# Last batch's ff stage: six of eight pairs of ff tiles by seven half-size products

## The chip, the core and the metric

The kernel runs on one core of one Trainium2 chip. The engines are PE (TensorE, with PEld for its weight loads), DVE (VectorE), ACT (ScalarE), POOL (GpSimd) and SP (SyncE, which here only issues DMAs). The metric is the device time in microseconds; lower is better. Three runs of the kernel before gave 210.69, 211.95 and 211.96 us, a median of 211.95.

## What is computed

Four batches of sparse attention (8 heads, 768 positions, head size 64), and on its output `x` (3072 x 512) an ff layer with a quick gelu:

```python
def _moe_ref(x, w_in, w_out):
    h = x @ w_in                               # 512 -> 2048
    g = h * (1.0 / (1.0 + np.exp(-1.702 * h)))
    return (g @ w_out).astype(np.float32)      # 2048 -> 512
```

Attention for each position: the keys within 15 positions, and the maximum of each block of 32 keys, against the values and the mean of each block of values.

## The kernel before, in words

The whole program is one list of words, `ORDER` (lines 35 to 110). A loop (lines 931 to 933) splits each word at its dots and calls the step of that name. Every engine is wrapped (`_Ordered`, line 18), so that each instruction is tied behind the one issued before it on its engine; line 28 is the helper's line and stands for nearly all instructions in the profile. The order on each engine's queue is thus meant to be the order of the words.

The stages of the four batches overlap: while PE computes the output products of batch b, the attention of batch b+1 is woven between them, and then the ff stage of batch b+1 follows. The words that matter here:

- `lk.b.h` (line 190): POOL issues the load of one head of keys. `lq` and `lv` do so for queries and values.
- `xk.s.g.e` (line 649): SP issues a DMA transpose of half of a group of four heads of keys into `kx`; it needs the four loads of that group. `xq` does so for queries.
- `v.b.half.p` (line 674): attention values of two heads. `nn.half.g` (line 697) normalizes four heads on DVE into `x2`, and `d.half.g` (line 715) has SP transpose them by DMA into `xTT[half][g]`, the ff input of positions `half` and model columns `g` (256 each). Each half has 384 positions.
- `f.half.nt.k...` (line 721): ff matmuls of tile nt (128 of 2048 ff columns), one for each `ko` named (`k0123`); ko 0 and 1 read `xTT[half][0]`, 2 and 3 `xTT[half][1]`. All are 128x128 by 128x384. `g.half.nt` (line 737) is the gelu on ACT into `gTb`.
- `gs.j.n.what` (line 740): sums and differences of gelu outputs, on DVE, or on POOL with `.g`.
- `p.t.what` (line 829): the output layer by seven half-size products, each 8 matmuls of 256 columns, with tiles named poA, poB and poC. `x.t.what` (line 852) takes a product out of PSUM, on ACT (`.a`) or DVE (`.d`; additions always on DVE). `o.t.half...` (line 869) has SP store a finished row block. `osb` has three buffers.
- `gate.2` (line 909): POOL copies one column of `xTT[1][1]`, so that loads behind it on POOL's queue wait for that transpose.
- `U`, `W`, `P`, `S`, `H`, `P7` (lines 751 to 814): an ff stage by seven products. In the kernel before only `P7.0` is in the list, which closes the pool `even` (attention buffers of even batches, line 425 onward) at the very end; the others are defined and not used.

The ff stage of each batch, the last too, is 16 tiles x 2 halves x 4 ko = 128 matmuls. PSUM has four single banks (0 to 3) and two double ones (`40`/`41`, `50`/`51`; `42` and `52` mean both halves).

Of the kernel before, what the change touches and what calls it, by code (L numbers as in the profile page):

```python
# [82 lines left out]
f.0.0.k23 lk.3.6 g.0.1 g.0.9 g.0.8 f.1.1.k0123.0 f.1.8.k0123.1 g.0.0 f.1.9.k0123.3 g.1.1 g.1.9 g.1.8 f.1.0.k0123.2
f.0.10.k0123.0 g.0.10 gate.2 g.1.0 gs.0.2.2 xk.1.1.0 f.1.2.k0123.1 gs.0.2.0.d gs.0.2.1 xk.1.0.1 f.1.10.k0123.3 g.1.2
o.1.1.1.0.2 g.1.10 lq.3.6 f.0.2.k0123.2 gs.0.2.3 lv.3.5.1 f.1.3.k0123.1 vm.3.52 g.1.3 xk.1.1.1 g.0.2 xk.1.0.0
o.1.2.1.0.2 f.0.13.k0123.0 f.0.3.k0123.2 f.1.11.k0123.3 f.0.12.k0123.1 g.0.3 g.0.13 g.1.11 xa.0.1 f.0.4.k0123.2 xq.1.1
f.1.12.k0123.3 lq.3.1 f.0.11.k0123.0 g.0.4 gs.2.2.2.g g.0.12 f.1.5.k0123.1 g.0.11 lq.3.2 vb xa.1.1 xq.1.0 f.0.5.k0123.2
g.1.5 g.1.12 ha.3.3.0 f.1.4.k0123.0 kR.1.d g.1.4 f.1.14.k0123.3 g.0.5 f.1.6.k0123.1 g.1.14 gs.2.2.0 ha.3.1.0
f.0.14.k0123.0 gs.2.2.1.g f.0.6.k0123.2 g.1.6 f.1.13.k0123.3 g.0.14 f.1.7.k0123.1 f.0.15.k0123.0 g.1.13 g.0.6 ka.1.d
f.1.15.k0123.3 f.0.7.k0123.2 s.3.0.1.42 gs.2.2.3 g.1.7 gs.6.1.0 gs.6.1.1 g.1.15 gs.4.2.0 g.0.15 gs.6.1.3 s.3.0.0.52  # L90
sd.3.1.0 g.0.7 gs.6.1.2 p.0.2.3 gs.7.1.0 p.0.1.2 X ha.3.0.0 e.0.1 p.1.2.0 e.0.0 x.0.1.d m.0.1 gs.7.1.1.g p.0.5.1
s.3.0.2.52 e.0.2 gs.4.2.1 x.0.5.d s.3.0.3.42 e.0.3 p.0.6 x.0.2.a gs.4.2.2 p.1.1.3 x.0.6.d s.3.1.1.42 gs.7.1.2 gs.7.1.3
s.3.1.0.52 gs.4.2.3 e.1.0 p.0.7 x.1.1.d p.0.3 ha.3.2.0 e.1.1 m.0.2 s.3.1.3.42 e.1.3 s.3.1.2.52 p.1.6 x.1.2.a x.0.3.a
m.0.0 x.0.7.a m.1.3 m.0.3 sd.3.0.0 p.1.5.1 v.3.0.2.40 e.1.2 v.3.0.0.50 v.3.0.3.41 v.3.0.1.51 o.2.0.0.0.2 G x.1.6.a m.1.2
p.0.4 p.1.7 m.1.0 x.0.4.a nn.0.0 x.1.5.d m.1.1 x.1.7.a p.2.1.2 p.1.3 nn.0.1 o.2.0.1.0.2 x.2.1.d p.1.4 d.0.0 v.3.1.2.40
v.3.1.3.41 x.1.3.a v.3.1.0.50 v.3.1.1.51 x.1.4.d d.0.1 p.2.5.1 p.2.6 nn.1.0 nn.1.1 x.2.6.a o.2.1.0.0.2 x.2.5.d p.2.2.3
x.2.2.a p.2.7 x.2.7.a p.2.3 p.2.4 f.0.1.k01.0 x.2.4.a f.0.1.k23 f.0.9.k01.3 f.0.0.k01.2 x.2.3.a f.0.9.k23 f.0.8.k01.1
f.0.0.k23 f.0.8.k23 o.2.1.1.0.2 g.0.9 g.0.0 g.0.8 d.1.0 d.1.1 f.1.9.k0123.3 f.1.0.k0123.2 g.0.1 f.1.8.k0123.1
f.1.1.k0123.0 g.1.9 g.1.0 f.0.2.k0123.2 f.1.11.k0123.3 g.1.8 g.0.2 f.1.2.k0123.1 g.1.1 f.0.10.k0123.0 g.1.11
f.1.13.k0123.3 g.1.2 f.1.3.k0123.1 g.0.10 f.0.3.k0123.2 g.1.13 f.1.10.k0123.3 g.0.3 f.0.11.k0123.0 f.0.4.k0123.2 g.1.3  # L100
g.1.10 f.1.12.k0123.3 o.2.2.0.0.2 gs.2.2.0.d g.0.4 g.0.11 f.1.4.k0123.1 gs.2.2.1.g g.1.12 f.0.12.k0123.0 f.1.14.k0123.3
o.2.2.1.0.2 g.0.12 gs.0.2.0.d f.0.5.k0123.2 g.1.4 f.1.5.k0123.1 f.0.13.k0123.0 g.0.5 f.0.6.k0123.2 gs.2.2.2.g g.1.5
g.0.13 g.1.14 f.1.6.k0123.1 f.0.14.k0123.0 g.0.6 g.1.6 gs.6.1.0.d f.0.7.k0123.2 g.0.7 gs.0.2.2.g gs.4.2.0.g
f.1.7.k0123.1 g.0.14 f.1.15.k0123.3 g.1.7 gs.0.2.1.g f.0.15.k0123.0 gs.4.2.1 g.0.15 gs.6.1.1 gs.6.1.2.d gs.2.2.3 p.0.1.2
g.1.15 gs.7.1.0 gs.7.1.1.g p.0.5.1 x.0.1.d p.0.2.0 p.0.6 x.0.6.a x.0.2.a gs.6.1.3 gs.4.2.2.d x.0.5.d gs.7.1.2 p.1.1.3
p.0.7 p.2.2.0 x.0.7.a x.1.1.a gs.0.2.3.d gs.7.1.3.g gs.4.2.3 p.0.4 x.0.4.a p.0.3 x.0.3.a p.1.2.2 x.1.2.a p.1.6
o.3.0.0.0.2 x.1.6.a p.1.5.1 x.1.5.d o.3.0.1.0.2 p.2.1.2 x.2.1.d p.1.3 x.2.2.a p.1.7 x.1.3.a p.2.6 x.2.6.d x.1.7.a
# [6 lines left out]
def kernel(  # L114
# [633 lines left out]

    seven = {}

    def seven_pool(n):
# [4 lines left out]
        seven["pool"] = p7
        seven["w"] = p7.tile([128, 4, 2, n * 128], F16, name="ws7", tag="ws7", bufs=1)
        seven["x"] = p7.tile([128, 4, 2, HALF], F16, name="xs7", tag="xs7", bufs=1)

    def w_sum7(what, j0, n, eng):  # L760
        c = slice(j0 * 128, (j0 + n) * 128)
        d = slice(d_ff // 2 + j0 * 128, d_ff // 2 + (j0 + n) * 128)
# [12 lines left out]
    def product7(j, what, where=None):  # L775
        c = slice(j * 128, j * 128 + 128)
        d = slice(d_ff // 2 + j * 128, d_ff // 2 + j * 128 + 128)
        w, x = seven["w"], seven["x"]
        lhs, rhs, name = {
            1: (w_in_sb[:, 0:2, c], xTT[0][0], "A"),  # L780
            2: (w_in_sb[:, 2:4, c], xTT[0][1], "C"),
            6: (w[:, 1, :, c], x[:, 1], "A"),
            5: (w[:, 0, :, c], x[:, 0], "B"),
            7: (w[:, 2, :, c], x[:, 2], "A"),
            3: (w[:, 3, :, c], xTT[1][1], "B"),
            4: (w_in_sb[:, 2:4, d], x[:, 3], "A")}[what]
# [8 lines left out]
    def taken7(j, what, eng):  # L795

        ph = seven[j, "at", what]
        if what in (1, 6, 5):
            if what == 1:
                seven[j, "h"] = seven["pool"].tile([128, 2, HALF], F32, name="h7", tag="h7")  # L800
            if what == 5:
                seven[j, "r"] = seven["pool"].tile([128, HALF], F32, name="r7", tag="r7")
            copy(eng, {1: lambda: seven[j, "h"][:, 0], 6: lambda: seven[j, "h"][:, 1],
                       5: lambda: seven[j, "r"]}[what](), ph)
# [159 lines left out]
```

## Time and profile before

| | |
|---|---|
| median of 3 runs | 211.95 us (210.69 to 211.96) |
| the profiled execution's own time | 211.7 us |
| its span | 210.0 us |
| PE busy | 200.4 us, 95% |
| DVE, ACT, POOL busy | 130.8, 114.3, 109.1 us |
| ff stage of batch 2 (PE) | from 123.10 us |
| ff stage of batch 3, the last (PE) | 167.26 to 188.06 us |
| output products of the last batch (PE) | 188.06 to 206.42 us |

The page of a profile gives busy time for each engine, the chain of work that ended last, and groups of instructions with their count, busy time, mean duration and the idle time before them with what ended it. A name such as `ph<-xT,w_in_sb` is output from inputs. In a timeline a row holds the start, the length and the number of like instructions; `SPq` and `POOLq` rows are the issuing of DMAs. Consecutive matmuls overlap, so their pace is read from the length of a run of them, not from the mean of one. The chain's rows are start, length, engine and tile.

### The profile page before, as it was taken

To read this page: it belongs to the slowest core of one execution; us is meant where nothing else is said; L and a number is where in the kernel's file an instruction comes from. 1 tells how busy PE (TensorE), PEld (TensorE's weight loads), DVE (VectorE), ACT (ScalarE), POOL (GpSimd) and SP (SyncE) were. 2 spreads that over 40 slices of the span, in tenths; PEclk is the share of its full clock that TensorE was granted. 3 is DMA by queue.
4 is the path that set the end of the run, shared out by engine and by line. 5 is a ranking of instruction groups with operands and counts; after the bars stand their busy time and mean duration, and the time that the engine had idled before them with its cause. 6 is when DMAs were issued, how large, how long until landed. Compare 5 with 4: busy or idle time off the path is not lost.

```text
span 210.0 us, 5880 instructions
## 1 busy us (share of the span) xinstructions
PE 200.4 (95%) x2440; PEld 145.8 (69%) x2440; DVE 130.8 (62%) x311; ACT 114.3 (54%) x227; POOL 109.1 (52%) x157
## 2 busy tenths in 40 slices
PE   7998798999999999999999999999999999999993
PEld 5656554667887886556788865657888865668882
DVE  5577873798997871168997822694888500166342
ACT  2473885659666736676764336567670157671100
POOL 7999972399982998448949422431000000863000
PEclk9999999999999999999999999999999999999998
DMA  4999999999999999999999999939215920000214
GB/s 67 162 166 189 209 213 221 182 144 122 99 134 199 156 177 183 130 126 141 148 166 204 142 227 180 187 29 169 50 53 139 160 105 0 0 3 0 100 53 150
DMA packets 96458, 27.74 MB, mean 132 GB/s; under 512 B 85024, under 2 KB 93488, under 8 KB 96432
## 3 DMA queue, kind: packets, MB, share of 16 engines
q0 software_dynamic: 70800, 13.64, 82.7%
q1 hardware_dynamic: 25632, 13.74, 33.2%
...
q14 instruction: 7, 0.06, 0.1%
...
## 4 chain that ended last, share of the span: by engine, by line
PE 79%; POOL 12%; DMA 5%; issue 1%; DVE 1%; SPq 0%; POOLq 0%; DVEq 0%
PE ph L28 36%; PE poA L28 19%; PE poB L28 10%; PE poC L28 5%; PE ps_s L28 3%; PE ps_av L28 3%; DMA vw<-vw 2%; POOL mk L28 2%; DMA out_dram<-osb 2%; POOL v0n L28 2%; POOL w_in_sb L28 2%; POOL kb L28 2%; POOL kx L28 2%; POOL qb L28 1%; PE ps_t L28 1%
## 5 line engine op out<-in xcount | busy, mean ns | idle before, releaser
L28 PE MATMUL ph<-xT,w_in_sb 128*128 128x384 f16 x512 | 86.1, 326 | 0.4 <-DVE osb L28 0.4
L28 ACT ACTIVATE gT<-ph 128x384 f16<-128x384 f32 x128 | 56.1, 495 | 30.6 <-PE ph L28 29.9
L28 PEld LDWEIGHTS <-w_in_sb 128*128 128x128 f16 x512 | 49.2, 98 | 32.4 <-issue 0.9
L28 PEld LDWEIGHTS <-gs 128*128 128x128 f16 x384 | 36.5, 98 | 4.6
L28 DVE TENSOR_TENSOR gs<-gT 128x768 f16<-128x768 f16 (+1 forms) x36 | 17.5, 498 | 29.1 <-ACT gT L28 29.0
L28 POOL TENSOR_TENSOR gs<-gs,gT 128x768 f16<-128x768 f16 (+1 forms) x6 | 8.8, 1461 | 41.8 <-PE ph L28 32.7
...
L28 ACT ACTIVATE a_sb<-ps_s 128x768 bf16<-128x768 f32 x32 | 24.8, 808 | 9.5 <-PE ps_s L28 9.3
L28 PEld LDWEIGHTS <-gT 128*128 128x128 f16 x288 | 27.3, 98 | 3.6
...
L28 PE MATMUL poA<-ws,gs 128*128 128x256 f16 x192 | 24.8, 273 | 0.0
...
L28 DVE TENSOR_TENSOR a_sb<-a_sb,mk 128x768 bf16<-128x768 bf16 x28 | 14.7, 550 | 3.0 <-ACT a_sb L28 2.2
L28 DVE TENSOR_TENSOR x<-ps_av,rc 128x768 f16<-128x768 f32 (+1 forms) x18 | 15.6, 869 | 0.6
L28 ACT ACTIVATE s<-poA 128x256 f32<-128x256 f32 x14 | 5.4, 382 | 19.3 <-PE poA L28 18.6
L28 PE MATMUL poB<-ws,gs 128*128 128x256 f16 x96 | 12.5, 273 | 0.0
L28 PE MATMUL poC<-w_out_sb,gT 128*128 128x256 f16 x96 | 12.5, 273 | 0.0
L28 PE MATMUL poA<-w_out_sb,gT 128*128 128x256 f16 x96 | 12.4, 273 | 0.0
L28 PE MATMUL poB<-w_out_sb,gs 128*128 128x256 f16 x96 | 12.4, 273 | 0.0
L28 PE MATMUL poA<-ws,gT 128*128 128x256 f16 x96 | 12.3, 273 | 0.0
L28 DVE TENSOR_REDUCE ka<-kx 128x48 bf16<-128x1536 bf16 x4 | 7.0, 1750 | 7.4 <-DMA kx<-kb 7.4
...
## 6 DMA issues: line engine op xcount, KB each, us to landing
...
kb<-in_k_dram POOLq DMA_DIRECT2D x24, 96.0 KB, 6.0
qb<-in_q_dram POOLq DMA_DIRECT2D x24, 96.0 KB, 5.0
...
```

What stands on the lines that cost most here:

```text
L28: r = f(*a, **kw)
```

## The change

In the last batch's ff stage the tiles 2 to 7 are paired with 10 to 15. With `w_in` and the input each cut in four quarters, the four quarter blocks of a pair's output (two tiles, two halves) come from seven products of half the depth (two ko) instead of eight. Each product is two matmuls of 128x384, so a pair takes 14 matmuls instead of 16. Tiles 0, 1, 8 and 9 stay as they were.

- `P7.6.2` closes `even` and opens the pool `seven` (weights sums `ws7`, input differences `xs7`, three `r7` buffers of 384 f32). It stands in batch 2's ff stage now, and the `P7.0` at the end is gone.
- `W.0` to `W.3`: the sums of quarters of `w_in` for the six pairs, 128 x 1536 f16, on DVE; three in batch 2's ff stage and one in batch 3's attention.
- `U.0` to `U.3`: differences of the inputs, 128 x 768 f16, on DVE, at the start of the last ff stage.
- For each pair j: `P.j.1` opens the left part of a double bank X, `P.j.5` its right part. `S.j.1` copies the left part from PSUM into another PSUM bank A (DVE); `P.j.2` is then added onto the left part by PE, `P.j.6` onto A. `S.j.5` (ACT) copies the right part to SBUF (h). `S.j.6` (DVE) writes A + h onto the right part in PSUM, and `P.j.3` is added onto that; `P.j.7` is added onto A, `S.j.7` (DVE) adds A to h, and `P.j.4` is added onto A. The gelus: `H.j.0` over both parts of X (768), `H.j.1` over A, `H.j.2` over h (384 each).
- The eight `gs` sums of the last batch that were on POOL are on DVE.
- The list of words from the end of batch 1's output products on is in another order, also for batch 2's ff stage and batch 3's attention, though with the same steps.

```diff
-    def seven_pool(n):
+    def seven_pool(n, j0):
         even.close()
         if not n:
             return
-        p7 = ctx.enter_context(tc.tile_pool(name="seven", bufs=2, side="right", reuse_waits="tile"))
+        p7 = ctx.enter_context(tc.tile_pool(name="seven", bufs=1, side="right", reuse_waits="tile"))
...
-        opens = where is not None
-        if opens:
-            seven[j, name] = bank(where, F32, "ph" + name)[:, 0:HALF]
-        seven[j, "at", what] = ph = seven[j, name]
+        if where is not None:
+            X = seven[j, "X"] = bank(where, F32, "phX")
+            seven[j, "l"], seven[j, "r"] = X[:, 0:HALF], X[:, 512:512 + HALF]
         for i in range(2):
-            pe.matmul(out=ph, lhsT=lhs[:, i], rhs=rhs[:, i], start=(opens and i == 0), stop=(i == 1),
-                      skip_group_check=True)
+            pe.matmul(out=seven[j, name], lhsT=lhs[:, i], rhs=rhs[:, i], start=(what in (1, 5) and i == 0),
+                      stop=(i == 1), skip_group_check=True)
...
+    def taken7(j, what, eng, where=None):
+        if what == 1:
+            seven[j, "A"] = bank(where, F32, "phA")[:, 0:HALF]
+            copy(eng, seven[j, "A"], seven[j, "l"])
+        elif what == 5:
+            seven[j, "h"] = seven["pool"].tile([128, HALF], F32, name="r7", tag="r7", bufs=3)
+            copy(eng, seven[j, "h"], seven[j, "r"])
         else:
-            t_ = {2: lambda: seven[j, "h"][:, 0], 3: lambda: seven[j, "h"][:, 1], 7: lambda: seven[j, "r"]}[what]()
-            dve.tensor_tensor(out=t_, in0=ph, in1=t_, op=ALU.add)
+            to = seven[j, "r"] if what == 6 else seven[j, "h"]
+            eng.tensor_tensor(out=to, in0=seven[j, "A"], in1=seven[j, "h"], op=ALU.add)
```

The words at the start of batch 2's ff stage, after the change (the last values of batch 2 are `v.2.1.3`):

```
... v.2.1.3.51 d.0.0 o.1.1.0.0.2 p.2.6 d.0.1 p.2.2.3 ... p.2.7 nn.1.0 f.0.1.k01.0 f.0.1.k23 nn.1.1 ... d.1.0
... f.0.9.k01.3 f.0.9.k23 p.2.4 d.1.1 o.1.2.0.0.2 ... f.0.8.k01.1 f.0.8.k23 lk.3.6 g.0.9 g.0.1 P7.6.2
xk.1.1.0 x.2.4.a f.1.9.k0123.3 f.0.0.k01.2 gate.2 xk.1.0.1 f.1.1.k0123.0 ...
```

and at the start of the last one (the last values of batch 3 are `v.3.1.3`):

```
... v.3.1.3.41 p.1.4 p.2.5.1 f.0.1.k01.0 nn.1.0 x.1.4.d x.2.6.a nn.1.1 f.0.1.k23 p.2.2.3 x.2.5.d o.2.1.0.0.2 o.2.1.1.0.2
d.1.0 p.2.3 p.2.7 g.0.1 x.2.2.a x.2.3.a U.0.d x.2.7.a P.2.1.42 f.0.8.k01.1 d.1.1 f.0.8.k23 P.2.5 P.3.1.52 P.3.5 g.0.8
U.2.d f.1.1.k0123.0 S.2.5.a U.1.d f.1.8.k0123.1 g.1.1 p.2.4 g.1.8 o.2.2.0.0.2 S.2.1.d.0 S.3.5.a U.3.d P.2.2 P.2.6
S.3.1.d.1 P.3.6 P.3.2 S.2.6.d P.2.3 S.3.6.d P.2.7 S.2.7.d f.0.9.k01.3 P.3.3 P.3.7 S.3.7.d x.2.4.a P.2.4 H.2.0 ...
```

On PE, DVE, ACT and POOL the built program follows the list. On SP it does not at one place, in batch 2: the instructions of SP's queue stand there in this order, before and after the change (`kx` in the group of heads 4 to 7 is `xk.1.1.0`, in heads 0 to 3 `xk.1.0.1`):

```
before: d.0.0  o.1.1.0  d.0.1  d.1.0     d.1.1  o.1.2.0   xk.1.1.0  xk.1.0.1  o.1.1.1  xk.1.1.1  xk.1.0.0  o.1.2.1  xq  xq
after:  d.0.0  o.1.1.0  d.0.1  xk.1.1.0  d.1.0  xk.1.0.1  d.1.1     o.1.1.1   o.1.2.0  xk.1.1.1  xk.1.0.0  o.1.2.1  xq  xq
```

In both programs `xk.1.1.0` waits for the semaphore that `lk.3.6` raises when it has landed, and `lk.3.6` stands at the same place of POOL's queue. PE's queue has 24 instructions fewer: 12 matmuls and 12 weight loads.

More of the change, by code (lines that the diff above doesn't have):

```diff
@@ L83 @@
[L83 to L107, printed above, removed]
@@ new lines @@
+xk.1.1.0 x.2.4.a f.1.9.k0123.3 f.0.0.k01.2 gate.2 xk.1.0.1 f.1.1.k0123.0 g.0.8 W.0.2.6.d g.1.1 f.1.8.k0123.1 lq.3.6
+g.1.9 W.2.2.6.d f.0.0.k23 f.0.10.k0123.0 f.1.10.k0123.3 g.1.8 lv.3.5.1 o.1.1.1.0.2 lq.3.1 g.0.0 f.1.2.k0123.1 xk.1.1.1
+f.1.0.k0123.2 g.1.10 g.0.10 g.1.2 xk.1.0.0 o.1.2.1.0.2 f.1.11.k0123.3 f.0.11.k0123.0 lq.3.2 g.1.0 g.1.11 g.0.11
+f.0.4.k0123.2 xq.1.1 xa.0.1 f.0.12.k0123.1 g.0.4 f.1.12.k0123.3 g.0.12 g.1.12 f.0.3.k0123.2 g.0.3 f.1.3.k0123.1 xq.1.0
+f.1.4.k0123.0 f.0.2.k0123.2 g.1.3 g.1.4 g.0.2 f.1.5.k0123.1 f.0.13.k0123.0 xa.1.1 vm.3.52 g.1.5 g.0.13 f.0.5.k0123.2
@@ new lines @@
+f.1.13.k0123.3 ka.1.d ha.3.3.0 f.0.15.k0123.0 g.0.5 gs.2.2.0 W.1.2.6.d gs.2.2.2.g f.0.6.k0123.2 kR.1.d g.0.15 g.1.13
+f.1.6.k0123.1 gs.0.2.2 f.1.14.k0123.3 ha.3.1.0 g.0.6 g.1.6 vb g.1.14 gs.6.1.2 f.0.7.k0123.2 gs.4.2.0 gs.6.1.0
+f.1.7.k0123.1 gs.2.2.1.g g.1.7 gs.4.2.1 gs.2.2.3 f.1.15.k0123.3 f.0.14.k0123.0 sd.3.1.0 gs.0.2.0.d s.3.0.0.52 g.1.15
+gs.6.1.1 s.3.0.1.42 g.0.7 p.0.1.2 g.0.14 ha.3.0.0 gs.7.1.0 x.0.1.d p.0.5.1 X e.0.0 gs.7.1.1.g p.0.2.3 e.0.1 gs.0.2.1
+p.0.6 gs.7.1.2 gs.6.1.3 s.3.1.0.52 ha.3.2.0 gs.4.2.2 e.1.0 x.0.2.a x.0.5.d s.3.0.3.42 p.1.2.0 gs.4.2.3 p.1.1.3
@@ new lines @@
+s.3.0.2.52 W.3.2.6.d e.0.3 gs.0.2.3 m.0.0 x.0.6.d sd.3.0.0 e.0.2 s.3.1.1.42 gs.7.1.3 x.1.1.d m.0.3 p.0.3 x.0.3.a e.1.1
+p.0.7 m.1.0 s.3.1.3.42 s.3.1.2.52 e.1.2 x.0.7.a p.1.5.1 o.2.0.0.0.2 e.1.3 p.1.6 p.0.4 m.0.1 m.0.2 m.1.1 v.3.0.2.40
+v.3.0.3.41 m.1.3 x.0.4.a x.1.5.d v.3.0.0.50 x.1.2.a v.3.0.1.51 o.2.0.1.0.2 x.1.6.a nn.0.0 p.2.1.2 p.1.7 G x.2.1.d nn.0.1
+m.1.2 x.1.7.a p.1.3 p.2.6 x.1.3.a v.3.1.2.40 v.3.1.0.50 d.0.0 v.3.1.1.51 d.0.1 v.3.1.3.41 p.1.4 p.2.5.1 f.0.1.k01.0
+nn.1.0 x.1.4.d x.2.6.a nn.1.1 f.0.1.k23 p.2.2.3 x.2.5.d o.2.1.0.0.2 o.2.1.1.0.2 d.1.0 p.2.3 p.2.7 g.0.1 x.2.2.a x.2.3.a
@@ new lines @@
+U.0.d x.2.7.a P.2.1.42 f.0.8.k01.1 d.1.1 f.0.8.k23 P.2.5 P.3.1.52 P.3.5 g.0.8 U.2.d f.1.1.k0123.0 S.2.5.a U.1.d
+f.1.8.k0123.1 g.1.1 p.2.4 g.1.8 o.2.2.0.0.2 S.2.1.d.0 S.3.5.a U.3.d P.2.2 P.2.6 S.3.1.d.1 P.3.6 P.3.2 S.2.6.d P.2.3
+S.3.6.d P.2.7 S.2.7.d f.0.9.k01.3 P.3.3 P.3.7 S.3.7.d x.2.4.a P.2.4 H.2.0 P.4.1.42 P.4.5 H.3.0 H.2.1 S.4.5.a P.3.4
+S.4.1.d.0 H.3.1 P.5.1.52 P.5.5 P.4.2 H.2.2 P.4.6 S.5.5.a f.0.9.k23 S.5.1.d.1 P.5.6 S.4.6.d g.0.9 H.3.2 P.5.2 P.4.3 P.4.7
+S.5.6.d f.0.0.k01.2 S.4.7.d P.5.3 H.4.0 P.5.7 P.4.4 P.6.1.42 gs.2.2.0 H.5.0 S.5.7.d P.6.5 H.4.1 P.7.1.52 S.6.5.a P.5.4
@@ new lines @@
+H.5.1 S.6.1.d.0 f.0.0.k23 P.7.5 g.0.0 gs.2.2.2 S.7.1.d.1 P.6.6 H.4.2 P.6.2 f.1.0.k0123.2 S.7.5.a gs.2.2.1 H.5.2 S.6.6.d
+g.1.0 P.7.6 P.7.2 S.7.6.d P.6.7 P.6.3 f.1.9.k0123.3 P.7.3 gs.4.2.0 H.6.0 S.6.7.d P.7.7 P.6.4 gs.0.2.2 g.1.9 S.7.7.d
+gs.4.2.1 gs.0.2.0 H.7.0 H.7.2 gs.6.1.2 H.6.1 H.6.2 p.0.1.2 x.0.1.d P.7.4 H.7.1 p.1.1.3 gs.6.1.0 gs.4.2.3 gs.7.1.0
+p.0.2.0 x.0.2.a p.0.5.1 gs.7.1.1 gs.0.2.1 gs.6.1.1 gs.0.2.3 gs.4.2.2 gs.7.1.3 p.2.2.0 gs.2.2.3 x.1.1.a gs.7.1.2 p.0.6
+x.0.5.d o.2.2.1.0.2 gs.6.1.3 x.0.6.a p.1.6 p.0.7 p.0.3 x.0.7.a p.0.4 x.0.3.a x.0.4.a p.1.5.1 p.1.2.2 x.1.2.a x.1.6.a
@@ L110 @@
+x.1.5.d o.3.0.0.0.2 o.3.0.1.0.2 p.1.7 x.1.7.a p.2.1.2 p.1.3 x.2.1.d p.2.6 x.1.3.a o.3.1.0.0.2 p.2.5.1 x.2.6.d x.2.5.a
+p.2.7 p.2.3 x.2.2.a p.1.4 x.2.7.a o.3.2.1.1.2 p.2.4 x.2.3.a x.1.4.d o.3.2.0.0.2 o.3.1.1.0.2 x.2.4.d o.3.2.1.0.1
 """
@@ L754, in seven_pool, with w_sum7 @@
             return
-        p7 = ctx.enter_context(tc.tile_pool(name="seven", bufs=2, side="right", reuse_waits="tile"))
[L756 to L762, printed above, removed]
+        p7 = ctx.enter_context(tc.tile_pool(name="seven", bufs=1, side="right", reuse_waits="tile"))
+        seven["pool"], seven["j0"] = p7, j0
+        seven["w"] = p7.tile([128, 4, 2, n * 128], F16, name="ws7", tag="ws7")
+        seven["x"] = p7.tile([128, 4, 2, HALF], F16, name="xs7", tag="xs7")
+    def w_sum7(what, j, n, eng):
+        c = slice(j * 128, (j + n) * 128)
+        d = slice(d_ff // 2 + j * 128, d_ff // 2 + (j + n) * 128)
         a11, a12, a21, a22 = (w_in_sb[:, 0:2, c], w_in_sb[:, 2:4, c], w_in_sb[:, 0:2, d], w_in_sb[:, 2:4, d])
-        w = seven["w"][:, :, :, c]
+        w = seven["w"][:, :, :, (j - seven["j0"]) * 128:(j + n - seven["j0"]) * 128]
         a, b, op = ((a21, a22, ALU.add), (w[:, 0], a11, ALU.subtract), (a11, a21, ALU.subtract),
@@ L777, in product7 @@
         d = slice(d_ff // 2 + j * 128, d_ff // 2 + j * 128 + 128)
-        w, x = seven["w"], seven["x"]
+        o = slice((j - seven["j0"]) * 128, (j - seven["j0"]) * 128 + 128)
+        w, x = seven["w"][:, :, :, o], seven["x"]
         lhs, rhs, name = {
[L780 to L785, printed above, removed]
+            1: (w_in_sb[:, 0:2, c], xTT[0][0], "l"),
+            2: (w_in_sb[:, 2:4, c], xTT[0][1], "l"),
+            6: (w[:, 1], x[:, 1], "A"),
+            5: (w[:, 0], x[:, 0], "r"),
+            7: (w[:, 2], x[:, 2], "A"),
+            3: (w[:, 3], xTT[1][1], "r"),
@@ L795, in taken7 @@
[L795 to L804, printed above, removed]
-        else:
-            t_ = {2: lambda: seven[j, "h"][:, 0], 3: lambda: seven[j, "h"][:, 1], 7: lambda: seven[j, "r"]}[what]()
-            dve.tensor_tensor(out=t_, in0=ph, in1=t_, op=ALU.add)
+            pe.matmul(out=seven[j, name], lhsT=lhs[:, i], rhs=rhs[:, i], start=(what in (1, 5) and i == 0),
+                      stop=(i == 1), skip_group_check=True)
@@ L809, in gelu7 @@
     def gelu7(j, which):
         k2 = j + NT // 2
-        o, i = ((gTb[:, j], lambda: seven[j, "h"].rearrange("p a c -> p (a c)")),
-                (gTb[:, j, 0:HALF], lambda: seven[j, "h"][:, 0]), (gTb[:, j, HALF:S], lambda: seven[j, "h"][:, 1]),
-                (gTb[:, k2, 0:HALF], lambda: seven[j, "A"]), (gTb[:, k2, HALF:S], lambda: seven[j, "r"]))[which]
+        o, i = ((gTb[:, j].rearrange("p (h c) -> p h c", h=2),
+                 lambda: seven[j, "X"].rearrange("p (h c) -> p h c", h=2)[:, :, 0:HALF]),
+                (gTb[:, k2, 0:HALF], lambda: seven[j, "A"]), (gTb[:, k2, HALF:S], lambda: seven[j, "h"]))[which]
@@ L856, in taken @@
             name = {1: "s1", 6: "s2", 5: "s5"}[what]
-            p_ = seven.get("pool", snap) if what == 1 else snap
-            t_ = now[t, name] = p_.tile([128, N1], F32, name=name, tag=name)
+            t_ = now[t, name] = snap.tile([128, N1], F32, name=name, tag=name)
             copy(eng, t_, po)
```

10 lines of the change are left out of this document (4 added, 6 removed).

## Prediction, on record before the change was run

> **What bounds the kernel now.** I read the page first (busy shares, chain), then the chain of waits by time, then busy time by window, and last the timelines of SP, POOL and PE around the edges of the ff stages.
>
> ```profile
> span 210.0 us, 5880 instructions
> PE 200.4 (95%) x2440; PEld 145.8 (69%) x2440; DVE 130.8 (62%) x311; ACT 114.3 (54%) x227; POOL 109.1 (52%) x157
> PE 79%; POOL 12%; DMA 5%; issue 1%; DVE 1%; SPq 0%; POOLq 0%; DVEq 0%
> ```
>
> ```profile
> 161.04 0.88 PE ps_av L28 x48
> ...
> 166.39 0.87 PE poA L28 x8
> 167.26 20.80 PE ph L28 x128
> 188.06 0.87 PE poA L28 x8
> ...
> 204.66 1.76 PE poA L28 x16
> 206.42 0.02 issue
> 206.44 0.42 DVE osb L28
> ```
>
> TensorE is the bound, and in the last batch it is the bound without a break. The chain's pieces join end to end: the last attention values end at 161.92 (call it V), six half-size output products follow, the 128 ff matmuls take 20.80 us (0.1625 us each), and output products at 0.87 us per eight run to 206.42. A matmul removed there shortens the run by its 0.1625 us, if nothing makes PE wait.
>
> ```profile
> 145.00:165.00 20.00, 20.00 (x329) 17.09 (x322) 15.72 (x36) 10.29 (x16) 0.91 (x1) 1.00 0.43 108
> 167.30:188.10 20.80, 20.80 (x130) 12.58 (x129) 3.75 (x6) 13.56 (x31) 8.32 (x5) 1.00 0.09 30
> ```
>
> Columns are the window, its length, then busy time of PE, weight loads, DVE, ACT and POOL. In the last ff stage DVE is idle for 17 of 20.8 us, ACT for 7.
>
> **The change, part by part.** *Matmuls.* A pair of ff tiles takes 16 matmuls of 384 columns (two tiles, two halves, four ko), and by seven products 14. Six pairs save 12: 12 x 0.1625 = 1.95 us. All are on the path.
>
> *Work added beside them.* DVE gets a copy and two additions of 384 f32 for each pair, four differences of the inputs (U, 768 f16), four of w_in (W, 1536 f16), and the eight gelu sums that POOL did. ACT's four gelus per pair become one of 768, two of 384 and a copy of 384.
>
> ```profile
> L28 ACT ACTIVATE gT<-ph 128x384 f16<-128x384 f32 x32 | 14.0, 491 | 7.2 <-PE ph L28 7.2
> L28 DVE TENSOR_TENSOR gs<-gT 128x768 f16<-128x768 f16 x3 | 1.6, 552 | 11.4 <-ACT gT L28 11.4
> L28 DVE TENSOR_TENSOR gs<-gT 128x384 f16<-128x384 f16 x4 | 1.5, 384 | 6.2 <-ACT gT L28 6.2
> L28 DVE TENSOR_TENSOR osb<-poC,s 128x256 f32<-128x256 f32 x3 | 1.3, 425 | 1.5 <-PE poC L28 1.5
> ```
>
> ```profile
> L28 DVE TENSOR_TENSOR x<-ps_av,rc 128x768 f16<-128x768 f32 x4 | 3.8, 958 | 0.1
> ```
>
> ```profile
> L28 ACT ACTIVATE a_sb<-ps_s 128x768 bf16<-128x768 f32 x32 | 24.8, 808 | 9.5 <-PE ps_s L28 9.3
> ```
>
> A 384-column f32 operation out of PSUM lies between 0.425 (256) and 0.958 us (768), by a straight line 0.56. A PSUM target is in no row; I price it as an SBUF one. DVE: 18 x 0.56 + 4 x 0.55 = 12.3 us, plus 6 x 0.55 + 2 x 0.38 = 4.1 of sums: beside the 3.75 it has, about 20 us, spread over the 18.85 us stage and the product stage behind it. ACT: 6 x (0.81 + 3 x 0.49) + 8 x 0.49 = 17.6 us. Both fit, because two pairs run interleaved: while pair 3 copies, pair 2 multiplies. What is not covered is the start. PE reaches the product that needs U.0 after five output products and ten ff matmuls, V + 5 x 0.87 + 10 x 0.1625 = V + 6.0.
>
> ```profile
> 163.22 2.55 SPq L28 DMA_TRANSPOSE xT<-x  x2
> ```
>
> ```profile
> xT<-x SPq DMA_TRANSPOSE x1, 2.8
> ```
>
> ```profile
> xT<-x SPq DMA_TRANSPOSE x2, 3.6
> ```
>
> Input d.1.0 was issued at V + 1.3 and landed 2.8 us later, d.1.1 at V + 2.6 and 4.4 (the median of the two is 3.6). Now d.1.0 stands behind a store that needs x.1.4, itself behind nn.1.0: V + 2.1. It lands at V + 4.9 to 5.7, U.0 takes 0.55, and PE waits 0 to 0.35. D.1.1 follows at V + 3.3 and lands at V + 6.1 to 7.7; then DVE's U.2, U.1, S.2.1, U.3 and S.3.1 (0.55 each) end at V + 8.9 to 10.5, and P.3.6, which needs the last, stands 18 ff matmuls and one output product behind U.0's product, at V + 9.8: 0 to 0.7. Together, since the second wait shrinks by the first, 0 to 0.9; I take 0.35. W.0 and W.2 (0.93 us each, on the line through 0.38 and 0.55) fall into a DVE gap of 6.7 us (row below); W.1 and W.3 lie where DVE has a fifth of its time free, 0. If that cover were gone, W.3 would cost its 0.93.
>
> *The SP queue, which the diff does not show.* In the built program the d.1.0 and d.1.1 transposes of batch 2 no longer stand ahead of the key transposes of batch 3: the order is d.0.1, xk.1.1.0, d.1.0, xk.1.0.1, d.1.1. And xk.1.1.0 waits for the last key load, lk.3.6. This is a new wait, and behind it in SP's queue stand both ff inputs of batch 2, two output stores and the other key transposes; POOL's gate.2, with three loads behind it, waits for d.1.1.
>
> ```profile
> 116.74 0.89 POOL L28 DMA_DIRECT2D kb<-in_k_dram  x1
> ...
> 118.58 3.91 SPq L28 DMA_TRANSPOSE xT<-x  x3
> ...
> 123.10 8.61 PE L28 MATMUL ph<-xT,w_in_sb 128*128 128x384 f16 x52 [0.41 <-DVE osb L28]
> ...
> 123.41 0.34 SPq L28 DMA_DIRECT2D out_dram<-osb  x1
> ...
> 124.36 3.33 SPq L28 DMA_TRANSPOSE kx<-kb  x2
> 124.58 0.19 POOL L28 CAST gate<-xT 128x1 bf16<-128x1 f16 x1 [6.95 <-DMA xT<-x]
> ...
> 130.05 1.03 DVE L28 TENSOR_TENSOR gs<-gT 128x768 f16<-128x768 f16 x2 [6.67 <-ACT gT L28]
> ```
>
> ```profile
> kb<-in_k_dram POOLq DMA_DIRECT2D x1, 96.0 KB, 5.1
> ```
>
> ```profile
> xT<-x SPq DMA_TRANSPOSE x1, 4.6
> ```
>
> ```profile
> L28 SPq DMA_TRANSPOSE xT<-x x4: 1211/1244/1257, 114.0 to 121.3; - x4
> ...
> DMA to landing us min/median/max: 3.2/4.3/5.7
> ```
>
> ```profile
> L28 SPq DMA_TRANSPOSE kx<-kb x4: 1217/1438/1939, 124.4 to 130.0; - x4
> ```
>
> The durations min/median/max are in ns. The first of the three transposes from 118.58 landed 4.6 us after its issue, the last 3.2. Before: d.1.1 was issued at 121.25 and landed 3.2 us later, 124.45 (the gate opened at 124.58), ahead of its first use at 123.10 + 16 x 0.1625 = 125.70. So it was hidden by 1.2 us. After: lk.3.6 keeps its place on POOL, was issued at 116.74 and lands 5.1 later, 121.84. Then xk.1.1.0, d.1.0, xk.1.0.1 hold SP for 1.44 + 1.24 + 1.44 us (medians) and three small steps of 0.05: d.1.1 is issued at 126.15 and lands at 129.35, by its own 3.2. PE now has only 12 ff matmuls ahead of the tile that needs it, and that tile's two first ko use d.1.0. The same amount of work was done before at 125.70 - 4 x 0.1625 + 2 x 0.1625 = 125.38. PE stands until 129.4: 4.0 us later, the former 0.41 wait included. Nothing gives it back, since PE is the bound from there to the end. Low end: 1.22, 1.21, 1.22 on SP and a landing of 2.8 (last batch): 128.5, 3.1 us. The key transposes come earlier for no gain, since PE sets when the next scores run. High end: SP was free at 123.75 before its first key transpose and began it at 124.36, so 0.6 more, then 1.94, 1.26, 1.94 and 4.6: 132.4, 7.0 us. I take 4.0, by the median rows.
>
> *The end* (206.42 to the profiled execution's 211.7 us) keeps its order: 0.
>
> **Sum:** 211.7 - 1.95 + 0.35 + 4.0 = 214.1. The profiled execution is 0.25 us below the median of 211.95, so against that median 214.35; I forecast **214.3 us**, 1.1% slower.
>
> **Rivals.** *The transposes stay hidden* (other side). Lk.3.6 lands so early that SP does not stand: the place is xk.1.1.0 on SP, the price of the wait 0, and the 0.41 goes too: 211.95 - 1.95 + 0.35 - 0.41 = 209.95. The point from which it decides: the sum turns at a shift of 1.6 us, d.1.1 landed by 127.0, lk.3.6 by 119.4. Against it: issued at 116.74, it would have to land within 2.7 us, and the quickest key load took 3.7.
>
> ```profile
> DMA to landing us min/median/max: 3.7/6.0/9.1
> ```
>
> *The clock falls in the hole.* PE would stand from about 124.5 until d.1.0 lands (issued at 123.4, 126.6), run two matmuls, and stand 2.5 us more.
>
> ```profile
> 1.30 4.45 PE L28 MATMUL ps_h<-warm 128*128 128x256 bf16 x20 [1.30 <-DVE warm L28]
> ...
> 34.69 0.73 PE L28 MATMUL ps_av<-vw,a_sb 128*64 128x65 bf16 x35 [0.77 <-DMA vw<-vw]
> ```
>
> At the start 256-column matmuls took 4.45 / 20 = 0.22 us where eight take 0.87 later, 0.109 each: twice as long for 4.45 us, a loss of 2.27. Later the longest single wait shown is 0.77 and leaves the rate alone. If the hole brings the slow rate back for as long, 214.3 + 2.3 = 216.6. [...]
>
> *The pairs are not covered.* A slow PSUM-to-PSUM copy, or ACT late with a gelu that frees a bank, costs each of six pairs 0.35 us (0.56 against 0.33 of matmuls beside it, and a hand-over): 214.3 + 2.1 = 216.4. For it: ACT at 17.6 of 18.85 us. Against: DVE has three steps per pair against 2.3 us of matmuls.
>
> *The change does not do what it says:* the built program has 12 matmuls and 12 weight loads fewer, so no.
>
> **How the numbers follow.** Main case 0.70 (by the bounds 211.95 - 1.95 + 0 + 3.1 = 213.1 to 211.95 - 1.95 + 0.9 + 7.0 = 217.9); hidden 0.10; clock 0.12; pairs 0.08. About 1% is what a measurement of this kernel can tell from no change: 209.83 and 214.07. Of the main case 0.42 lies above 214.07 and 0.28 within; clock and pairs lie above; of the hidden case 0.06 is within and 0.04 below. Faster 0.04, same 0.34, slower 0.62. The range, 211.5 to 217.5, takes in a shift half hidden, and leaves out the hidden case and the uppermost tenth.
>
> **What would show it.** Right: in the profile after, SP's timeline has a kx transpose between the second and third xT, waiting for kb; PE waits 3 to 5 us for xT near 125 to 129; the last ff stage shows 32 ph matmuls and 84 of the seven products in about 19 us; DVE's pair operations near 0.56. Wrong: PE without a gap near 125 (hidden), matmuls of 0.33 us behind it (clock), or PE waits spread over the last stage (pairs).

## The result, and the profile after

The changed kernel took 219.8 us (median; 218.82 to 221.87), the kernel before beside it 211.95: a ratio of 1.039 with a 95% interval of 1.0298 to 1.0482. It is slower by 3.9%, and above the predicted range. The profiled execution took 218.82 us, 7.1 more than that of before, and its span is 7.1 longer. Here and below, a time in us is the median of all runs, while a ratio compares only runs within 1.5% of the fastest of their kernel, because some executions of one and the same kernel are slower (35 of the kernel before took 210.16 to 215.09 us).

The page of the changed kernel, and below it the clock row of the kernel before:

```profile
span 217.1 us, 5904 instructions
PE 201.6 (93%) x2428; PEld 144.9 (67%) x2428; DVE 147.0 (68%) x344; ACT 117.2 (54%) x227; POOL 98.8 (46%) x150
PEclk9999999999999999999999975999999999999999
PE 71%; DMA 14%; DVE 6%; issue 3%; SPq 2%; ACT 1%; POOL 1%; DVEq 0%; POOLq 0%
L28 PE MATMUL ph<-xT,w_in_sb 128*128 128x384 f16 x416 | 75.0, 334 | 4.1 <-DMA xT<-x 4.1
```

```profile
PEclk9999999999999999999999999999999999999998
```

TensorE has its 12 matmuls fewer (2440 before) and is busy 1.2 us longer. Two things on this page tell why: the ff matmuls waited 4.1 us for input transposes, and the row of the granted clock (in tenths, for 40 slices of the span), 9 in the kernel before up to its last slice, has a 7 and a 5. The timeline of PE shows both (start, length, then in brackets the idle time before and what ended it):

```profile
125.19 0.81 PE L28 MATMUL ph<-xT,w_in_sb 128*128 128x384 f16 x4
128.38 0.82 PE L28 MATMUL ph<-xT,w_in_sb 128*128 128x384 f16 x2 [2.38 <-DMA xT<-x]
130.45 14.35 PE L28 MATMUL ph<-xT,w_in_sb 128*128 128x384 f16 x74 [1.25 <-DMA xT<-x]
...
168.20 0.95 PE L28 MATMUL ps_av<-vw,a_sb 128*64 128x65 bf16 x48
```

And the same stretch by windows (start and end, length, busy time of PE, weight loads, DVE, ACT, POOL, then the granted clock):

```profile
128.00:130.00 2.00, 0.82 (x2) 0.28 (x3) 0.00 (x0) 0.00 (x0) 0.00 (x0) 0.51 0.89 152
130.00:132.00 2.00, 1.55 (x5) 0.69 (x5) 0.00 (x0) 0.00 (x0) 1.19 (x3) 0.50 1.01 302
132.00:134.00 2.00, 2.00 (x8) 0.96 (x7) 0.00 (x0) 0.80 (x2) 2.00 (x3) 0.50 1.32 137
134.00:136.00 2.00, 2.00 (x11) 1.05 (x10) 0.00 (x0) 1.06 (x3) 0.16 (x1) 0.78 1.72 182
```

TensorE stops at 126.0, runs two matmuls, stops again and resumes for good at 130.45. The clock is at half from 128.0 to 134.9 (0.78 of the last two microseconds is 0.88 at half and 1.12 at full), so the 74 matmuls take 14.35 us; at 0.1625 each they would take 12.03. Along TensorE the 7.1 us add up as follows:

| stretch | before | after | shift |
|---|---|---|---|
| to the first matmul behind the hole, equal work | 125.38 | 130.45 | +5.07 |
| from there to the end of the last attention values (V) | 36.54 | 38.70 | +2.16 |
| from V to the last matmul's end | 44.48 | 44.67 | +0.19 |
| from there to the end of the span | 3.60 | 3.28 | -0.32 |

The third row is the change's own place. It is 12 matmuls shorter (-1.95) and got 2.1 us of new gaps. I count gaps from start to start: a group of n matmuls of 384 columns should be followed after n x 0.1625 us. The idle time in brackets is 0.16 less, since each matmul is drawn at twice its pitch (a mean of 326 ns on the page of before, where 128 in a row take 20.80 us, 162.5 ns each).

```profile
174.44 0.81 PE L28 MATMUL ph<-xT,w_in_sb 128*128 128x384 f16 x4
176.11 0.48 PE L28 MATMUL phX<-xs,ws 128*128 128x384 f16 x2 [0.86 <-DVE xs L28]
...
184.81 0.48 PE L28 MATMUL phX<-xT,w_in_sb 128*128 128x384 f16 x2 [0.20 <-DVE phA L28]
...
186.12 0.48 PE L28 MATMUL phA<-xs,ws 128*128 128x384 f16 x2 [0.18 <-DVE phA L28]
```

The first product that needs U.0 starts 1.67 us after four matmuls that take 0.65: a gap of 1.02. One of 0.31 ahead of P.3.6 follows, then 0.37 and 0.35 where TensorE waits for the first-product copy, and one of 0.11. DVE's timeline shows what the copies wait for:

```profile
175.50 0.56 DVE L28 TENSOR_TENSOR xs<-xT,xT 128x768 f16<-128x768 f16 x1 [1.56 <-DMA xT<-x]
...
184.19 0.57 DVE L28 COPY phA<-phX 128x384 f32<-128x384 f32 x1 [0.94 <-ACT r L28]
185.50 0.57 DVE L28 COPY phA<-phX 128x384 f32<-128x384 f32 x1 [0.75 <-ACT r L28]
```

U.0 (`xs`) waits for the transpose d.1.0. The copies wait for ScalarE's copy `r` out of the same PSUM tile `phX`, though neither writes it: in the built program the two reads come one behind the other (E4 below turns them round).

### The profile page after: what moved, and what is told of

Read it like the earlier page. It is cut to its first block, busy times and chain, and to the rows that moved or that the text cites. A ratio compares the mean times of both kernels' runs of the same rounds, so it can differ in the third digit from the quotient of the medians.

```text
span 217.1 us, 5904 instructions
## 1 busy us (share of the span) xinstructions
PE 201.6 (93%) x2428; PEld 144.9 (67%) x2428; DVE 147.0 (68%) x344; ACT 117.2 (54%) x227; POOL 98.8 (46%) x150
## 4 chain that ended last, share of the span: by engine, by line
PE 71%; DMA 14%; DVE 6%; issue 3%; SPq 2%; ACT 1%; POOL 1%; DVEq 0%; POOLq 0%
PE ph L28 27%; PE poA L28 15%; PE poB L28 8%; DMA out_dram<-osb 6%; PE poC L28 4%; DMA xT<-x 3%; PE ps_av L28 3%; PE ps_s L28 3%; PE phX L28 3%; SPq L28 2%; PE phA L28 2%; DMA vw<-vw 2%; DMA qb<-in_q_dram 2%; PE ps_t L28 1%; DVE x L28 1%
## 5 line engine op out<-in xcount | busy, mean ns | idle before, releaser
L28 PE MATMUL ph<-xT,w_in_sb 128*128 128x384 f16 x416 | 75.0, 334 | 4.1 <-DMA xT<-x 4.1
L28 ACT ACTIVATE gT<-ph 128x384 f16<-128x384 f32 x104 | 46.8, 496 | 38.7 <-PE ph L28 37.8
L28 PEld LDWEIGHTS <-w_in_sb 128*128 128x128 f16 x452 | 44.0, 99 | 34.4 <-issue 5.7
L28 DVE TENSOR_TENSOR gs<-gT 128x768 f16<-128x768 f16 (+1 forms) x39 | 20.3, 535 | 6.4 <-ACT gT L28 6.4
L28 DVE TENSOR_TENSOR gs<-gT,gs 128x768 f16<-128x768 f16 (+1 forms) x20 | 10.6, 539 | 0.1
```

The lines of the kernel that those rows point to most:

```text
L28: r = f(*a, **kw)
```

## The experiments

The main theory (A): the loss is a hole in the third batch, made by the order on SP's queue, and the slow clock behind it; the seven products by themselves save 1.95 us and lose about as much in waits at their own stage. The rivals: the seven products, their sums or their PSUM operations cost it; or the new order of the words costs it in another way than by the transposes.

**E1, e1_pool_opened_earlier.** The words on SP keep the list's order except around the place where the pool is opened, so this moves that place alone, by 29 words (the expectation's "twelve" is a miscount):

```diff
-v.2.1.3.51 d.0.0 ... lk.3.6 g.0.9 g.0.1 P7.6.2 xk.1.1.0
+v.2.1.3.51 P7.6.2 d.0.0 ... lk.3.6 g.0.9 g.0.1 xk.1.1.0
```

> Only edit: the word that opens the pool for the seven products stands right behind batch 2's last values, twelve words earlier; SP's queue then has d.1.0 and d.1.1 ahead of the key transposes again, all else as in the changed kernel. Theory A (the order on SP made the loss: 5.1 us of hole in PE and 2.2 us of matmuls at the halved clock behind it): no hole near 126 to 130, granted clock 1.00 throughout, 212.3 us, within 211.5 to 213. Rival B (the seven products and their sums cost the time): 217 us or more. Rival C (the hole without the clock is all that SP makes): about 214.5.

Measured: 213.12 us, 1.0081 [1.0038, 1.0123], with d.1.0 and d.1.1 ahead of the key transposes and the clock at 1.00 in the profiled execution. That one word is worth 6.7 of the 7.9 us. What TensorE still waits for from 118 us on (total, times, longest):

```profile
PE ph L28 <- DMA xT<-x: 1.4, 1, 1.4
PE phX L28 <- DVE xs L28: 0.9, 1, 0.9
PE phX L28 <- DVE phA L28: 0.2, 1, 0.2
PE phA L28 <- DVE phA L28: 0.2, 1, 0.2
```

**E2, e2_before_with_sp_order.** The converse, with no seven products at all: the kernel before, with the five words behind `lk.3.6`.

```diff
-... lv.3.4.0 d.1.0 lv.3.2.1 ... G d.1.1 o.1.2.0.0.2 ... lk.3.6 ... gate.2 g.1.0 gs.0.2.2 xk.1.1.0 ... xk.1.0.1
+... lv.3.4.0 lv.3.2.1 ... G ... lk.3.6 xk.1.1.0 d.1.0 xk.1.0.1 d.1.1 o.1.2.0.0.2 ... gate.2 g.1.0 gs.0.2.2 ...
```

> The kernel before with one edit: d.1.0 and d.1.1 of batch 2 stand behind the key transposes on SP as in the changed kernel (xk.1.1.0, d.1.0, xk.1.0.1, d.1.1), no seven products. Theory A: a hole in PE until about 130 and then half clock, 5 + 2.2 us: 219 us (217 to 220). Rival B (the products cost the time): within 1 us of 212.

Measured: 217.71 us, 1.0269 [1.021, 1.0329], 5.8 us over the kernel before. PE's timeline, then two windows:

```profile
127.61 0.50 PE L28 MATMUL ph<-xT,w_in_sb 128*128 128x384 f16 x2 [2.04 <-DMA xT<-x]
129.67 8.55 PE L28 MATMUL ph<-xT,w_in_sb 128*128 128x384 f16 x34 [1.56 <-DMA xT<-x]
```

```profile
128.00:130.00 2.00, 0.44 (x3) 0.16 (x2) 0.00 (x0) 0.00 (x0) 0.19 (x1) 0.67 0.92 244
...
134.00:136.00 2.00, 2.00 (x9) 0.99 (x8) 0.00 (x0) 0.38 (x1) 0.00 (x0) 0.62 1.90 202
```

So SP's order alone makes a hole and the slow clock behind it.

**E3, e3_hole_filled.** The changed kernel with products that nobody reads in both waits, so that TensorE stays busy and only the clock is taken away:

```diff
-f.1.9.k0123.3
+Z.13.2 f.1.9.k01.3 Z.9.2 f.1.9.k23
```

> The changed kernel, with 13 and 9 matmuls of 384 columns of no use placed in the hole, ahead of d.1.0's and of d.1.1's first use, into a bank that is free there: they add work that the output does not use. Theory A with the clock as its own term: PE goes on at the same 130.4 us, the granted clock stays 1.00, and the 2.2 us behind the hole go: 217.6 us (217 to 218.5). [...]

Measured: 216.55 us, 1.0222 [1.0171, 1.0274], 3.2 us under the changed kernel; the clock stays at 1.00 in and behind the hole. The clock row of its page comes first, then the matmuls behind the hole:

```profile
PEclk9999799999999999999999999999999999999999
```

```profile
131.47 12.19 PE L28 MATMUL ph<-xT,w_in_sb 128*128 128x384 f16 x74
```

The same 74 matmuls take 12.19 us instead of 14.35: 2.16 us is what the clock cost behind the hole. TensorE does not resume earlier (131.47; SP was 1 us later here), so the hole itself stays. The profiled execution ends 2.0 us earlier than that of the changed kernel: it resumes 1.0 later, wins 2.16 by the clock, and does not have the wait of 0.86 for U.0. The rest of the 3.2 us between the medians is not explained. The 7 in the row is another fall of the clock, far from the hole, from 23.8 to 27.2 us in the first batch; the last section comes back to it. By 118 us this execution is level with the changed kernel again (SP issues d.0.1 at 118.71, there at 118.86).

**E9 and E10, one of the two waits filled.** `Z.13.2 f.1.9.k01.3 f.1.9.k23` and `f.1.9.k01.3 Z.9.2 f.1.9.k23`.

> The changed kernel with 13 products that nobody reads (into PSUM bank 2) in the first of the two waits only, so that TensorE is idle only in the second, of about 1.3 us (the two useful products between the waits stay). For the clock: if one short idle stretch is not enough, the granted clock stays at 1.00 in 128 to 136 us, the 74 products behind the hole take 12.0 to 12.2 us, and the time falls by about 2.3 us, as with both filled. If any idle of over 1 us there lowers it: 0.50 over some 5 us behind the hole, 14 us for the 74 products.

> The same with 9 such products in the second wait only: TensorE is idle for about 2.4 us in the first, then works without a gap. If a single idle of 2.4 us lowers the clock: 0.50 over some 5 us from about 129 us. If it is the sum of the two idles (3.6 us in a stretch of 4.5 us) that lowers it: 1.00 throughout.

Measured: 217.18 and 219.34 us, one run each. In the first the clock stays at 1.00 over waits of 1.52 and 1.53 us:

```profile
123.96 1.14 PE L28 MATMUL ph<-xT,w_in_sb 128*128 128x384 f16 x6 [1.52 <-DMA xT<-x]
...
131.25 12.19 PE L28 MATMUL ph<-xT,w_in_sb 128*128 128x384 f16 x74 [1.53 <-DMA xT<-x]
```

In the second, TensorE happened to wait 2.19 us earlier, for d.0.1, and only 0.89 in the place meant. So the run did not test what it was made for, but shows something else: behind this one wait the clock halves, behind a later one of 1.70 it does not.

```profile
124.88 1.76 PE L28 MATMUL ph<-xT,w_in_sb 128*128 128x384 f16 x6 [2.19 <-DMA xT<-x]
...
133.76 11.54 PE L28 MATMUL ph<-xT,w_in_sb 128*128 128x384 f16 x70 [1.70 <-DMA xT<-x]
```

```profile
124.00:126.00 2.00, 1.12 (x5) 0.60 (x5) 0.79 (x1) 0.00 (x0) 0.00 (x0) 0.81 0.13 13
126.00:128.00 2.00, 2.00 (x10) 1.28 (x9) 0.00 (x0) 0.87 (x2) 0.00 (x0) 0.50 1.11 67
128.00:130.00 2.00, 1.21 (x6) 0.48 (x4) 0.00 (x0) 0.87 (x2) 0.00 (x0) 0.84 0.69 134
132.00:134.00 2.00, 0.30 (x3) 0.17 (x2) 0.00 (x0) 0.00 (x0) 0.14 (x1) 1.00 0.84 218
```

**E5 and E6, the two halves of what E1 leaves.** E5 has the order before up to the last ff stage and the seven products there; E6 has the new order up to there and the ordinary ff stage of before.

```diff
 E5, the kernel before's list:
+P7.6.2  behind v.2.1.3.51;  W.0.2.6.d W.2.2.6.d  behind G;  W.1.2.6.d W.3.2.6.d  ahead of X
-the last stage's words    +those of the changed kernel
```

> The kernel before, with its own order of words up to the last batch's ff stage, and the changed kernel's order from there on; the pool opened right behind the last PV tile of the third batch (no broken pins), the four sums of weights put into VectorE's two idle stretches. So the seven products without the rest of the new order. Theory A (the list's transposes and the clock are the loss, the seven products by themselves gain 1.95 us of products and lose about 2.1 us of waits at the start of the stage and at the copies): 211.5 to 212.5 us, the clock at 1.00 throughout, waits of about 0.9 for the first sum and 0.2 to 0.4 for the copies. Rival (the seven products cost more than their own waits, by the output products after them or by the sums of weights): over 213.3 us. Rival (the waits are hidden when the order ahead is the old one): 210.2 us.

> The converse: the new order of words up to the last batch's last PV tile, without the sums of weights and the pool, and the kernel before's ff stage of the last batch (sixteen products per pair). Nothing of the seven products is in it. Theory (the new order's own cost is the 1.4 us wait of the third batch's first ff tiles for the transpose d.0.1): 212.9 to 213.4 us, with that wait in the trace and no other. Rival (the order costs nothing and what the kernel with the pool opened earlier loses lies in the seven products): 211.7 to 212.2 us.

Measured: 212.46 us, 1.0026 [0.9987, 1.0064], and 213.49 us, 1.0051 [1.0004, 1.0097]. Together +0.8%, which is E1's +0.8%, though each is known only to about 0.4%. E5's clock was not at 1.00 throughout, as was expected, but at half from 23.0 to 26.4 us; its five runs with a mean clock of 0.992 have a median of 212.16 us and the other seven 212.73, so this did not cost it time. TensorE's waits from 118 us on, in E5 and then in E6:

```profile
PE phX L28 <- DVE xs L28: 0.9, 1, 0.9
PE ph L28 <- DVE osb L28: 0.4, 1, 0.4
PE phX L28 <- DVE phA L28: 0.2, 1, 0.2
PE phA L28 <- DVE phA L28: 0.2, 1, 0.2
```

```profile
PE ph L28 <- DMA xT<-x: 1.0, 1, 1.0
PE poB L28 <- DVE s L28: 0.5, 1, 0.5
```

The 0.4 for `osb` is in the kernel before too (0.41). Without the queue's fault the seven products end level: their 1.95 us go into 2.2 us of gaps at their own stage (1.09, 0.31, 0.36, 0.34 and 0.11, by starts). The new order of the words costs about one us of its own, mostly at an input transpose (d.1.1 in E6's profile, d.0.1 in E1's).

**E4, e4_start_and_copies.** E1 with d.1.0 ahead of a store, x.2.7 ahead of U.0, and DVE's copy ahead of ScalarE's for pairs 3 to 7 (`-S.j.5.a ... S.j.1.d.b  +S.j.1.d.b S.j.5.a`).

> As the first kernel, and in the last ff stage: d.1.0 goes on SP ahead of the store o.2.1.1, the addition x.2.7 ahead of U.0 on DVE, and for pairs 3 to 7 the copy S.j.1 (DVE) stands ahead of S.j.5 (ACT), so that it no longer waits for ACT to have read the other half of the same PSUM tile. Theory A (the 2.1 us lost in that stage are 1.0 of start and 1.1 of copies that wait): 1.5 to 2 us under the first kernel, about 210.4. Rival D (the chain copy, product, addition is simply too long for two pairs in turn): no gain over the first kernel, 212.

Measured: 213.19 us, 1.0051 [1.0016, 1.0087], no gain over E1: a miss. The wait at the copies changed sides (0.3 us of PE for ScalarE's `r`), and d.1.0, issued earlier, landed 5 us later instead of 4.5. Which of the two reads comes first did not matter here; there must be other work for TensorE meanwhile.

**E7, E8, E11: order mended on the new list.** E7 has the third batch's p.2.4 and half of f.0.9 ahead of the second half of f.0.1; E8 adds cover in the last stage and other banks for the copies; E11 is E8 with more cover and with x.2.7 ahead of p.2.4 and S.3.1 ahead of P.3.2 again. E7, E8, E11 and E12 do not compute the same output as the kernel before. In E7 and E8 the third batch's x.2.7 takes poA with p.2.4 in it, and in E8 S.3.1 copies with P.3.2 already added. E11 and E12 have neither; their sums come out changed with the copies in banks 2 and 3, and not in E13, which differs from E12 in the banks alone. Why the banks matter is not shown. The number and shape of the instructions are those of a kernel with the right sums, so these four times speak for the schedule only, not for a kernel that can be used.

> The changed kernel with the pool opened earlier, and on TensorE in the third batch the output product p.2.4 and the first half of ff tile f.0.9 ahead of the second half of f.0.1, as the kernel before has them: 8 + 2 products of 1.37 us in all to cover the wait of 1.36 us for the transpose d.0.1. If the wait is a matter of order alone: 211.6 to 212.0 us, 1.0 to 1.4 under the 213.1 of the one without this edit. If the wait only moves (to d.1.1, or to the gelu tiles): 212.8 to 213.3 us.

> The edit of the third batch's order, and in the last batch: d.1.0 ahead of the store o.2.1.1, x.2.7 ahead of U.0, the output product p.2.4 as cover ahead of P.2.5 (0.88 us of work for the 0.88 us wait for the first sum), the copies S.2.1, S.4.1, S.6.1 into bank 3 instead of bank 0, and half tiles of f.0.9 and f.0.0 as cover ahead of P.4.2 and P.5.6. Theory (each wait is a matter of what stands next on TensorE): 210.2 to 211.0 us, under the kernel before by up to 1.7. Rival (the stage is paced by VectorE's chain of sums and copies, so that covered waits come back a pair later): 211.5 to 212.0 us, the same as with the third batch's order alone.

> The edits of both stages, with the order among one tile's readers and writers kept (x.2.7 ahead of p.2.4 in the third batch, S.3.1 ahead of P.3.2), and three more: p.0.2 ahead of p.0.5 in the third batch (0.88 us of work for the 0.59 us wait for the sums gs), and in the last batch ScalarE takes x.2.4 and S.3.5 ahead of g.1.1 (S.3.1 into bank 2), the half tile f.0.9 as cover behind P.3.6. Theory (each wait is a matter of what stands next on TensorE and ahead on ScalarE; 1.95 us fewer products then come out at the end): waits of TensorE from 118 us on under 0.8 us, span about 208.6 us, 0.990 to 0.997 of the kernel before. Rival (VectorE's chain of sums and copies paces the start of the stage): waits of 1.2 us or more there again, 0.998 to 1.003.

Measured: 212.34 us, 1.0007 [0.9971, 1.0043]; 212.52 us, 1.0022 [0.9984, 1.0059]; 212.41 us, 1.0042 [1.0013, 1.0071]. E7 missed its 211.6 to 212.0, E8 and E11 the gain that was expected of them: by the ratios the three lie 0.4 to 0.7% under E1, with intervals that overlap E1's, and none gets under the kernel before. On this list a covered wait comes back: in E8's profile as 0.6 us each at ScalarE's `r`, at the copies and at the sums gs, in E11's (its slowest run) as 1.36 us at d.0.1, which landed 7.1 us after its issue at 118.72 where E1's took 5.4 (from 117.80 to 123.18), 0.84 at the sums gs and 0.39 at `osb`, with nothing but one 0.18 in the last stage. So the last stage can be covered, but in these profiles the third batch gives the gain back. Why d.0.1 landed so late is not shown.

**E12 and E13: the old list with the mended stage.** E12 joins E5's list to E11's stage. E13 keeps the copies in the changed kernel's banks and moves the ordinary tiles out of their way; all sums are those of the changed kernel.

```diff
 E13, last stage, against the changed kernel:
-o.2.1.0.0.2 o.2.1.1.0.2 d.1.0     +o.2.1.0.0.2 d.1.0 o.2.1.1.0.2
-U.0.d x.2.7.a                     +x.2.7.a U.0.d
-P.2.5 ... g.1.1 p.2.4             +p.2.4 P.2.5
-f.1.1.k0123.0  f.1.8.k0123.1      +f.1.1.k0123.3  f.1.8.k0123.2
-S.2.5.a ... g.1.1 ... S.3.5.a     +S.2.5.a x.2.4.a S.3.5.a ... g.1.1
+S.3.1 ahead of U.3;  P.3.2 ahead of P.2.6;  half tiles of f.0.9 behind P.3.6 and
+ahead of P.4.2, of f.0.0 ahead of P.5.6
```

> The kernel before's own order up to the last ff stage (as in the run with the seven products alone) and the last stage as mended in the run beside this one. Theory: of the 1.3 us of waits that the last stage had there, 0.9 or more go: 0.992 to 0.998 of the kernel before, waits of TensorE from 160 us on under 0.4 us. Rival (as beside): no gain over the seven products alone, 1.000 to 1.005.

> As the run with the old order and the mended last stage, with the first-product copies where the changed kernel has them (S.2.1, S.4.1, S.6.1 in bank 0, the other three in bank 1), and the ordinary tiles f.1.1 in bank 3 and f.1.8 in bank 2 instead, so that the copies still need not wait for them. All sums of the pairs are those of the changed kernel. Theory (the waits are a matter of what stands next and of which bank): waits of TensorE from 160 us on under 0.5 us, against 1.3 with the seven products alone, and 0.990 to 0.998 of the kernel before. Rival (cover moves the wait a pair on): waits of 1.2 us again and 1.000 to 1.005.

Measured: 211.25 us, 0.9978 [0.9938, 1.0017], and 210.95 us, 0.9929 [0.9883, 0.9975]. E12 cannot be told from the kernel before. E13 beats both kernels. TensorE's waits from 118 us on in E13, and the only one of its last stage:

```profile
PE ph L28 <- DVE osb L28: 1.2, 1, 1.2
PE phA L28 <- DVE phA L28: 0.2, 1, 0.2
```

```profile
178.06 0.48 PE L28 MATMUL phA<-xs,ws 128*128 128x384 f16 x2 [0.18 <-DVE phA L28]
```

By starts the gaps of the stage are 0.93 us in all (five of 0.11 to 0.35), against 2.1 in the changed kernel: 1.95 - 0.93 = 1.0 us of the saving arrives. The time fell by 0.7% (0.25 to 1.2), which is 1.5 us (0.5 to 2.5) of 211.75; the medians of all runs are 0.8 us apart, so the size of the gain is known only roughly. More than half of the gaps of the stage were a matter of order and banks, not the price of seven products.

## Why the prediction was wrong

It named the right place and mechanism, and the direction, but put the cost at 2.4 us where it was 7.9. Three steps failed.

*The rival that was held apart came on top of the main case.* The clock in the hole had a chance of 0.12 and a price of +2.3. It did fall, and cost 2.16 behind the hole (E3). The price was right. The chance was too low, and the term stood outside the sum. The chance was the author's estimate: in the trace of before the longest wait but the start's was 0.77 us, so nothing there showed what the clock does in a hole of over 2 us. Here it fell at 128.06 us, 2.06 us into the first wait of 2.38 and ahead of the two matmuls; in E10 it fell 0.4 us behind a single wait of 2.19. Hole and clock together give 216.6 by the prediction's own numbers, still inside its range; the two terms below carry it out. Together: 214.3 + 2.16 (clock) + 1.07 (hole) + 1.75 (stage) - 0.3 (end) = 219.0, against 219.8 measured; the 0.8 left over is within the spread of the changed kernel's runs, whose profiled one took 218.82.

*The shift of the hole, 4.0 us, was 5.07.* The built order on SP, the wait of xk.1.1.0 for lk.3.6 and the place were as predicted; the sizes came out above the middle. The load and SP's queue in the changed kernel (POOL's issue, the load's KB and landing time, SP's timeline):

```profile
116.04 0.83 POOL L28 DMA_DIRECT2D kb<-in_k_dram  x1
```

```profile
kb<-in_k_dram POOLq DMA_DIRECT2D x1, 96.0 KB, 6.4
```

```profile
122.58 1.22 SPq L28 DMA_TRANSPOSE kx<-kb  x1
123.92 1.36 SPq L28 DMA_TRANSPOSE xT<-x  x1
125.87 1.44 SPq L28 DMA_TRANSPOSE kx<-kb  x1
127.41 1.46 SPq L28 DMA_TRANSPOSE xT<-x  x1
```

The load took 6.4 us instead of 5.1 and so landed at 122.44 instead of 121.84. SP began its first key transpose 0.7 later than predicted, and reached d.1.1 4.83 us after that instead of 4.26: a longer d.1.0, and half a microsecond of standing ahead of xk.1.0.1. D.1.1 landed 3.04 after its issue, as priced (3.2). The bounds (3.1 to 7.0) held.

*The start of the stage, 0.35 us, was 1.33 with 0.8 more at the copies.* The prediction let d.1.0 be issued at V + 2.1 and land 2.8 to 3.6 later. It was issued at V + 1.9 (171.01), behind the issue of two stores, and landed 4.5 later; the start's own bounds (0 to 0.9) were too narrow. The 0.8 us at the copies is a step that the prediction did not have: it let DVE and ScalarE read one PSUM tile at the same time, and priced only "ACT late with a gelu" as a rival. Two reads by two engines are in sequence in the built program, so 1.1 us pass between the pair's product and the end of its copy, and TensorE has 0.65 to 0.97 us of other work. E13's cover takes the gaps from 2.1 to 0.93 us in all.

*What was right.* The matmuls: 12 x 0.1625 went. The PSUM-to-PSUM operations, priced 0.56 with no row to go by:

```profile
L28 DVE COPY phA<-phX 128x384 f32<-128x384 f32 x6 | 3.4, 566 | 3.9 <-ACT r L28 2.7 <-ACT gT L28 1.1
L28 DVE TENSOR_TENSOR phX<-phA,r 128x384 f32<-128x384 f32 x6 | 3.4, 564 | 1.2 <-PE phX L28 1.2
```

566 and 564 ns. The rival "pairs not covered" does not hold as it was put: two of the six pairs wait, by 0.35 us each, not all six. W.0 to W.3 cost nothing: DVE did the first two while it had nothing else to do, and with E5's places for them TensorE's waits are the same. The end was 0.3 shorter.
